# A PSUM tile each for the transposed solution and the transposed output, and two fixed tiles for the solution

## The chip, the cores and the metric

The kernel runs on one core of a Trainium2 chip. The metric is the device time of one execution in microseconds. The kernel is timed as the median of three runs; the profile is of one more execution, taken by the hardware profiler.

## The reference

Three layers follow each other on float32 data of batch 4, sequence 768 and width 320 (8 heads of 40). Only the first is touched here: a recurrent attention whose state, one 40x40 matrix for each batch and head, is updated at each of the 768 positions. The second (a gated product with a convolution of three taps) and the third (a Fourier mix, a normalisation and two products) follow it on its output.

```python
for t in range(S):
    y[:, :, t] = np.einsum('bhd,bhde->bhe', rt, state)
    Sa = np.einsum('bhde,bhe->bhd', state, at)
    state_decay = state * wt[:, :, None, :] - np.einsum('bhd,bhe->bhde', Sa, bt)
    state = state_decay + np.einsum('bhd,bhe->bhde', vt, kt)
...
h = np.maximum(x @ w_in, 0.0)
...
return (h * gate @ w_out).astype(np.float32)
...
X = np.fft.fft(x, axis=1)
X = np.fft.fft(X, axis=2)
...
ch = np.maximum(un @ w_ch1, 0.0) @ w_ch2
```

## The kernel before

The attention works on chunks of 64 positions: 12 chunks `c` and 4 batches `b`, so 48 units, one after the other. Two batches share a set of loaded tiles (`hb` is the half, `bl` the batch in it), and the heads lie in three groups of up to three heads (120 partitions). Inside a chunk the recurrence is a triangular system. Its inverse `tt` is found for eight units at a time by `inverse`, most of it on DVE: a transpose (L311), then 60 operations that each need the one before them (L331 multiplies, L334 adds; "the chain" below), then three transposes (L341 once, L344 twice), after which TensorE merges blocks in two parts, `bp` (L358) and, a step later, `mp` (L371).

`run` (L593) calls `step` (L525) 52 times. In step `n` stand, in this order, parts of several units: `u` of unit n interleaved with `hu` of unit n-3's next chunk and with `y` of unit n-2 (L530 to L539); `stage_s` (`sp`, the new state) and `stage_g` (`gp`) of unit n-1; what is prepared ahead (`joins`, which issues `bp` and `mp`, then `gram` and `xp` of a unit 15 steps on, while there are any); `stage_sb` (`ss`); `stage_ut` of unit n; `stage_o` of unit n-3. The names are those of the PSUM tiles. All tiles of PSUM come from one pool of eight buffers, each a bank of 512 float32 a partition (`pst`, L133).

`stage_ut` (L428) transposes the solution `z` of the unit by three matmuls (128x64 results) into columns 0 to 191 of the tile `ct`, and ACT copies them to `zt` (L435). `stage_o` (L499) transposes the output `ys` of an older unit into columns 192 to 383 of the same `ct`, and DVE multiplies them into `xo` (L507), which is stored. TensorE's part of most of these stages goes through `in_turn` (L382), so that its order is that of the calls. A scheduler sets the order on the other engines as it builds the program, from its own estimate of times. It also makes two instructions of different engines on one tile of PSUM wait for each other, as in program order.

`load_z` (L178) takes a new `z` from a pool with two buffers for each chunk and half, loads its upper 64 partitions and clears 40 padding columns of the lower 64 on GpSimd (L183). ACT writes the solution into the lower half (L425).

Of the kernel before, what the change touches and what calls it, by code (L numbers as in the profile page):

```python
# [10 lines left out]
F32 = mybir.dt.float32  # L11
# [9 lines left out]
C = 64  # L21
NCH = S // C
NG = 3
HG = 3
P3 = HG * D
DM = H * D
# [48 lines left out]
def turns(left, right):  # L75


    sides = []
    for stages in (left, right):
        ops = []  # L80
        for todo, end in stages:
            ops += [(op, None) for op in todo[:-1]] + [(todo[-1], end)]
        sides.append(ops)
    n = max(len(ops) for ops in sides)
    for k in range(n):
        for ops in sides:
            for op, end in ops[k * len(ops) // n:(k + 1) * len(ops) // n]:
                op()
                if end is not None:
                    end()  # L90
                    yield
# [7 lines left out]
class Attn:  # L99
    def __init__(self, ctx, tc, ins, xd):  # L100
        self.tc, self.nc, self.xd = tc, tc.nc, xd
        self.i = ins
        nc = self.nc
        cp = ctx.enter_context(tc.tile_pool(name="a_const", bufs=1))
        self.early = ctx.enter_context(tc.tile_pool(name="a_early", bufs=1, side="right"))
        self.pre = ctx.enter_context(tc.tile_pool(name="a_pre", bufs=1))
        mid = [ctx.enter_context(tc.tile_pool(name=f"a_mid{j}", bufs=1)) for j in range(2)]
        self.ps = ctx.enter_context(tc.tile_pool(name="a_ps", bufs=8, space=PSUM))
        self.ends = cp.tile([P3, 6 * 66], F32, name="ends")
        nc.vector.memset(self.ends, 0.0)  # L110
        ev = self.ends.rearrange("p (a b) -> p a b", b=66)
        nc.vector.memset(ev[:, :, 0:66:65], 1.0)
        self.stat = cp.tile([P3, 4 * NCH], F32, name="stat")
        self.abd = [cp.tile([P3, HG, 2 * NG, C], F32, name=f"abd{j}") for j in range(2)]
        self.rbd = [cp.tile([P3, HG, 2 * NG, C], F32, name=f"rbd{j}") for j in range(2)]
        self.ident = cp.tile([128, 128], F32, name="ident")
        mlt = cp.tile([128, C + 2], F32, name="mlt")
        self.mlt, self.mq = mlt[:, 0:C], mlt[:, C:C + 2]
        self.mltq = mlt
        self.mdiag = cp.tile([P3, P3], F32, name="mdiag")  # L120
        self.hbd = [cp.tile([128, 4, 2, D], F32, name=f"hbd{b}") for b in range(B)]
        self.st = [cp.tile([P3, NG, P3], F32, name=f"st{b}") for b in range(B)]
        self.sb = [cp.tile([P3, NG, P3], F32, name=f"sb{b}") for b in range(B)]
        self.ys = [self.pre.tile([64, NG * P3], F32, name=f"ys{j}") for j in range(2)]
        self.sm = [self.pre.tile([P3, NG, P3], F32, name=f"sm{j}") for j in range(1)]

        self.slots = {}
        for k, n, m, shape in (("x", 10, 4, [128, 2, NG * P3]), ("lk", 8, 4, [128, 2, 4, C]), ("tt", 2, 1, [128, 32, 64])):
            self.slots[k] = [mid[j >= m].tile(shape, F32, name=f"{k}{j}") for j in range(n)]
        self.hf, self.late, self.markd, self.lastpe = {}, None, None, None  # L130
        self.grp = {}
# [46 lines left out]
    def load_z(self, c, hb):  # L178
        nc, pre, i = self.nc, self.pre, self.i
        d = self.hf[c, hb]  # L180
        z = d["z"] = pre.tile([128, 2, NG * P3], F32, name="z", tag="z", bufs=2)
        nc.sync.dma_start(z[0:C], i["zv"][c, hb])
        nc.gpsimd.memset(z[C:128, :, DM:], 0.0)  # L183
        zt = d["zt"] = pre.tile([P3, 6, 2, C], F32, name="zt", tag="zt", bufs=2)
        nc.sync.dma_start(zt[:, :, 0], i["vt"][c, hb])
        for h in range(HG):
            nc.sync.dma_start(self.rbd[hb][D * h:D * h + D, h], i["r"][c, hb, D * h:D * h + D])
# [3 lines left out]
        self.nc.sync.dma_start(t, self.i["r"][c, hb])  # L191

    def pads(self):
        for t in self.ys:
            self.nc.gpsimd.memset(t[:, DM:], 0.0)
        for t in self.sm:
            self.nc.gpsimd.memset(t[:, 2], 0.0)
# [227 lines left out]
            self.mark = nc.scalar.mul(d["z"][64:128, bl, 0:DM], hu[0:64, 0:DM], -1.0)  # L425
        return ops, end

    def stage_ut(self, c, b, ct):  # L428
        nc = self.nc
        bl, d = b % 2, self.hf[c, b // 2]  # L430
        up = ct[:, 0:192]
        for gi in range(NG):
            self.mm_t(up[0:P3, 64 * gi:64 * gi + 64],
                                d["z"][64:128, bl, P3 * gi:P3 * gi + P3], self.ident[64:128, 64:128])
        self.mark = nc.scalar.copy(d["zt"][:, bl * NG:bl * NG + NG, 1],  # L435
                       up[0:P3, 0:192].rearrange("p (g t) -> p g t", t=C))
# [59 lines left out]
            self.mm_t(ss[0:P3, P3 * gi:P3 * gi + P3], self.st[b][:, gi], self.ident[:P3, :P3])  # L496
        nc.scalar.copy(self.sb[b].rearrange("p a b -> p (a b)"), ss[0:P3, 0:NG * P3])

    def stage_o(self, c, b, ct):  # L499
        nc, pre = self.nc, self.pre  # L500
        bl, d = b % 2, self.hf[c, b // 2]
        yt = ct[:, 192:384]
        for gi in range(NG):
            self.mm_t(yt[0:P3, 64 * gi:64 * gi + 64], d["ys", b][:, P3 * gi:P3 * gi + P3],
                                self.ident[:64, :64])
        xo = pre.tile([P3, NG, C], F32, name="xo", tag="xo", bufs=3)
        self.markd = nc.vector.tensor_tensor(xo, yt[0:P3, 0:192].rearrange("p (g t) -> p g t", t=C),  # L507
                                d["wx"][:, bl * NG:bl * NG + NG, 0:C], op=ALU.mult)
        for x, c0 in self.xd:
            if c0 <= c < c0 + x.shape[-1] // C:  # L510
                nc.sync.dma_start(x[b].rearrange("(g p) t -> p g t", p=P3)[:, :, (c - c0) * C:(c - c0 + 1) * C], xo)
# [13 lines left out]
    def step(self, n, pre):  # L525
        def at(k):
            return divmod(n - k, B) if 0 <= n - k < B * NCH else (None, None)

        left, right = [], []
        c, b = at(0)  # L530
        if c is not None:
            left.append(self.stage_u(c, b))
        c, b = at(HL)
        if c is not None and c < NCH - 1:
            left.append(self.stage_h(c + 1, b))
        c, b = at(2)
        if c is not None:
            right.append(self.stage_y(c, b))
        yield from turns(left, right)  # L539
        c, b = at(1)  # L540
        if c is not None and c < NCH - 1:
            self.stage_s(c, b)
            yield
        if c is not None:
            self.stage_g(c, b)
            if b % 2 and c + 1 < NCH:
                self.load_z(c + 1, b // 2)
            yield
        for _ in pre:
            yield  # L550
        c, b = at(3)
        if c is not None and c < NCH - 1:
            self.stage_sb(c, b)
            yield
        ct = self.pst("ct")
        c, b = at(0)
        if c is not None:
            self.stage_ut(c, b, ct)
            yield
        c, b = at(3)  # L560
        if c is not None:
            self.stage_o(c, b, ct)
            yield


# [843 lines left out]
```

## Time and profile before

| | |
|---|---|
| median of three runs | 1041.9 us (1039.63 to 1045.36) |
| profiled execution | 1041.13 us; its span, first to last instruction, 1039.3 us |
| busy share of the span | PE 82%, DVE 64%, ACT 50%, POOL 42% |
| mean granted TensorE clock | 0.901 of full speed |
| attention's steps | 72.4 to 544.5 us of the span, then the other two layers |

PE is TensorE, PEld its weight loads, DVE VectorE, ACT ScalarE, POOL GpSimd, SP the queue that issues the loads and stores. A busy share is an average over the whole span, in which the steps of the attention and the large products after it have different limits. Idle time of an engine counts only where the chain of work passes through it. Each engine works through its own queue in order, so an instruction that waits holds back all that stand behind it.

### The profile page before, as it was taken

Reading aid. Unit: us, or ns where it says so; the run is one execution under the profiler, and the core shown is the slowest. Engines: PE = TensorE matmul, PEld = TensorE weight load, DVE = VectorE, ACT = ScalarE, POOL = GpSimd, SP = SyncE. Lnnn points to the kernel's source line nnn. Section 1 sums busy time; section 2 is a strip of 40 time slices with the busy share of each in tenths; the row PEclk is TensorE's granted clock in tenths of the full one; section 3 lists DMA queues with packets and bytes.
Section 4 is the critical chain, followed back from the end, with each engine's and each line's share of the span. In section 5 each row is a group of like instructions: output and inputs, shape, how many; then the busy total and the mean of one; then the engine's idle time right before and its main releaser. Section 6 shows DMA issues by size and latency. Waiting matters only on the chain. (4 is left out here: it accounts for less than half of the span.)

```text
span 1039.3 us, 21821 instructions
## 1 busy us (share of the span) xinstructions
PE 847.6 (82%) x8178; PEld 772.4 (74%) x8178; DVE 665.1 (64%) x1320; ACT 521.5 (50%) x1448; POOL 432.2 (42%) x529
## 2 busy tenths in 40 slices
PE   4557657657867776687878999988999999999997
PEld 3446657656766675677767777776888999999997
DVE  6984965983796597296326888888875445434321
ACT  4657466556556655544337676665754331222211
POOL 5555264453445344233316776767365203101000
PEclk8668688888887888897989999999999999999999
DMA  9523335445454435252834573321304000000001
GB/s 235 167 65 88 103 110 133 138 121 137 130 153 113 114 108 141 69 148 76 246 79 116 147 221 115 96 71 33 89 2 149 30 7 20 21 20 20 20 7 36
DMA packets 102990, 101.16 MB, mean 97 GB/s; under 512 B 47272, under 2 KB 89115, under 8 KB 102875
## 3 DMA queue, kind: packets, MB, share of 16 engines
q1 hardware_dynamic: 100907, 94.73, 32.5%
q0 software_dynamic: 1968, 4.93, 1.6%
q8 instruction: 67, 1.10, 0.5%
q14 instruction: 48, 0.39, 0.1%
HBM read 74.81 MB, written 20.76 MB: 92 GB/s over the span
## 5 line engine op out<-in xcount | busy, mean ns | idle before, releaser
L877 DVE SCALAR_TENSOR_TENSOR c<-h,cw,c 128x384 f32<-128x384 f32 x128 | 110.6, 867 | 23.7 <-ACT c L875 20.9
L894 PE MATMUL acc<-w_out_f,z 128*128 128x320 f32 x384 | 114.9, 436 | 5.7 <-POOL z L881 3.0
L386 PE MATMUL ct<-ident,ys 64*120 64x64 f32 x144 | 21.2, 262 | 116.3 <-ACT zt L435 116.0
L1131 DVE SCALAR_TENSOR_TENSOR gl<-hp,gh 128x384 fp32r<-128x384 f32 x80 | 44.4, 556 | 111.3 <-ACT gh L1130 111.2
L1130 ACT ACTIVATE gh<-hp 128x384 fp32r<-128x384 f32 x80 | 39.3, 492 | 149.8 <-PE hp L700 149.6
L386 PEld LDWEIGHTS ct<-ident,ys 64*120 64x120 f32 x144 | 13.8, 154 | 122.8 <-ACT zt L435 122.2
L894 PEld LDWEIGHTS acc<-w_out_f,z 128*128 128x128 f32 x384 | 71.2, 190 | 29.4 <-POOL z L881 4.7
L700 PE MATMUL hp<-xh,w_in_h 128*128 128x386 f32 x192 | 75.8, 395 | 11.1 <-ACT h L868 11.0
L700 PE MATMUL hp<-uh,w_ch_h 128*128 128x384 f32 x240 | 82.3, 343 | 0.0
L700 PE MATMUL hp<-ul,w_ch_h 128*128 128x384 f32 x240 | 81.0, 337 | 0.0
L386 PE MATMUL yp<-x,gt 128*64 128x40 f32 x768 | 76.6, 267 | 1.6 <-DVE gt L468 1.6
L1154 POOL DMA_INDIRECT out<-o,rows x12 | 11.8, 984 | 150.7 <-DVE o L1149 131.9
L386 PEld LDWEIGHTS yp<-x,gt 128*64 128x64 f32 x768 | 72.8, 171 | 2.2 <-DVE gt L468 2.2
L1144 PE MATMUL acc<-w_ch_h,gh 128*128 128x320 f32 x240 | 73.2, 312 | 0.0
L1144 PE MATMUL acc<-w_ch_l,gh 128*128 128x320 f32 x240 | 73.0, 309 | 0.0
L217 PE MATMUL gram<-abd,kb 120*128 120x192 f32 (+1 forms) x288 | 56.4, 339 | 17.0 <-DMA abd<-a 10.5
L334 DVE TENSOR_TENSOR A<-A,tmp 128x30 f32<-128x30 f32 (+9 forms) x150 | 65.5, 437 | 3.5
L331 DVE TENSOR_TENSOR tmp<-A 128x30 f32<-128x30 f32 (+9 forms) x150 | 64.8, 432 | 3.4
L700 PE MATMUL hp<-xl,w_in_h 128*128 128x386 f32 x192 | 66.4, 346 | 0.0
L217 PEld LDWEIGHTS gram<-abd,kb 120*128 120x128 f32 x288 | 51.5, 212 | 18.8 <-POOL l L262 10.7
L455 POOL TENSOR_TENSOR st<-st,sm 120x360 f32<-120x360 f32 x40 | 41.3, 1032 | 56.9 <-DVE sm L454 53.1
L237 POOL TENSOR_TENSOR lk<-lk,mlt 128x256 f32<-128x256 f32 x48 | 37.7, 786 | 61.3 <-ACT lk L236 60.9
(225 smaller groups left out, 2703.4 us busy)
## 6 DMA issues: line engine op xcount, KB each, us to landing
kb<-in_kb SPq DMA_DIRECT2D x24, 360.0 KB
vbd<-in_vbd SPq DMA_DIRECT2D x24, 320.0 KB
xd<-xo SPq DMA_DIRECT2D x56, 90.0 KB
w<-in_w SPq DMA_DIRECT2D x24, 185.6 KB
a<-in_a SPq DMA_DIRECT2D x24, 180.0 KB
z<-in_zv SPq DMA_DIRECT2D x24, 180.0 KB
zt<-in_vt SPq DMA_DIRECT2D x24, 180.0 KB
rbd<-in_r SPq DMA_DIRECT2D x72, 60.0 KB
```

What stands on the lines that cost most here:

```text
L217: nc.tensor.matmul(gp[:, 192 * gi:192 * gi + 64 * nh], d["kb"][:, bl * NG + gi].rearrange("p a b -> p (a b)"), abd[:, 0:nh, bl * NG + gi], ...
L237: nc.gpsimd.tensor_tensor(d["lk"][:, bl], d["lk"][:, bl], self.mlt.unsqueeze(1).to_broadcast([128, 4, C]), op=ALU.mult)
L331: nc.vector.tensor_tensor(tmp, A[:, s + 1:32, s:s + 1].to_broadcast([128, n, s]), A[:, s:s + 1, 0:s].to_broadcast([128, n, s]), op=ALU.mult)
L334: nc.vector.tensor_tensor(A[:, s + 1:32, 0:s], A[:, s + 1:32, 0:s], tmp, op=ALU.add)
L386: self.lastpe = op(*args, **kw)
L455: nc.gpsimd.tensor_tensor(self.st[b], self.st[b], t, op=ALU.add)
L700: nc.tensor.matmul(out, l, r, start=(j == 0), stop=(j == len(ops) - 1))
L877: nc.vector.scalar_tensor_tensor(c, h[:, j:HS + j], cw[:, f, j:j + 1], c, op0=ALU.mult, op1=ALU.add)
L894: nc.tensor.matmul(self.acc[t][:, 0:DM], z[:, ts], w[:, f], start=(f == 0), stop=(f == NF1 - 1))
L1130: self.mark = nc.scalar.activation(gh, hp[:, 0:HS], AF.Relu)
L1131: nc.vector.scalar_tensor_tensor(gl, hp[:, 0:HS], 0.0, gh.bitcast(F32), op0=ALU.max, op1=ALU.subtract)
L1144: nc.tensor.matmul(self.acc[t][:, 0:DM], l[:, ts], r, start=(f == 0 and j == 0), stop=(f == NF2 - 1 and j == 2))
```

## The change

The shared tile `ct` becomes two, `up` and `yt`, one for each stage. The tiles of `z` are two fixed ones, one for each half, whose padding is cleared once (`pads`) and no longer for each chunk and half.

```diff
+        self.z = [self.pre.tile([128, 2, NG * P3], F32, name=f"z{j}") for j in range(2)]
...
-        z = d["z"] = pre.tile([128, 2, NG * P3], F32, name="z", tag="z", bufs=2)
+        z = d["z"] = self.z[hb]
         nc.sync.dma_start(z[0:C], i["zv"][c, hb])
-        nc.gpsimd.memset(z[C:128, :, DM:], 0.0)
...
     def pads(self):
+        for t in self.z:
+            self.nc.gpsimd.memset(t[C:128, :, DM:], 0.0)
...
-    def stage_ut(self, c, b, ct):
+    def stage_ut(self, c, b):
...
-        up = ct[:, 0:192]
+        up = self.pst("up")
...
-    def stage_o(self, c, b, ct):
+    def stage_o(self, c, b):
...
-        yt = ct[:, 192:384]
+        yt = self.pst("yt")
...
-        ct = self.pst("ct")
```

In the attention the order on PE stays; what changes there is what its instructions wait for. This is PE's queue at the end of a step without a merge, before (the last row but one of a step's transposes is `ct<-ident,ys`, then the next step begins with `u`):

```order
L253 MATMUL xp<-ident,kb 128x120 x2
L386 MATMUL ss<-ident,st_103 120x120 [waits DVE_49]
L386 MATMUL ss<-ident,st_103 120x120 x2
L386 MATMUL ct<-ident,z 120x64 [waits Activation_49]
L386 MATMUL ct<-ident,z 120x64 x2
L386 MATMUL ct<-ident,ys_109 120x64 [waits Activation_49]
L386 MATMUL ct<-ident,ys_109 120x64 x2
L386 MATMUL u<-hbd_99,tt_130 64x80 [waits PE_49]
```

And the same place in the changed kernel (lines are two further down):

```order
L255 MATMUL xp<-ident,kb 128x120 x3
L388 MATMUL ss<-ident,st_103 120x120 x3
L388 MATMUL up<-ident,z_111 120x64 [waits Activation_49]
L388 MATMUL up<-ident,z_111 120x64 x2
L388 MATMUL yt<-ident,ys_109 120x64 [waits PE_49,Activation_49]
L388 MATMUL yt<-ident,ys_109 120x64 x2
L388 MATMUL u<-hbd_99,tt_132 64x80 [waits Activation_49]
```

Nothing moved. The wait of `ct<-ident,ys` on ACT was for the copy L435 of this same step; that of `yt` is for the bank that it takes over, which `hu` of this step held until ACT's copies of it (L410, in the new file L412). `u` takes the bank of `yp`, and waits for ACT's copy L487 (now L489) of this step.

The scheduler orders DVE anew. Here is the end of the third chain (that of `tt_129`) on DVE before, from the store's multiplication `xo` on; `bp` of this chain is issued on PE a step later:

```order
L331 TENSOR_TENSOR tmp<-A 128x30
L334 TENSOR_TENSOR A<-A,tmp 128x30
L507 TENSOR_TENSOR xo<-ct,wx 120x192
L164 SCALAR_TENSOR_TENSOR wx<-w,ends 120x396
L341 STREAM_TRANSPOSE t_3872<-A 128x32x32
L344 STREAM_TRANSPOSE tt_129<-A 128x32x32 x2
L163 RECIPROCAL ends<-vx 120x6
L450 TENSOR_TENSOR sm_110<-sp,mdiag 120x240
L454 TENSOR_TENSOR sm_110<-sp,mdiag 80x80
```

And the end of the same chain in the change (L313 for L311, L333, L336, L343, L346 for L331, L334, L341, L344), which now lies in the very step in which PE issues `bp`; `gt` of that step stands four rows ahead of the first row here:

```order
L336 TENSOR_TENSOR A<-A,tmp 128x5x26
L333 TENSOR_TENSOR tmp<-A 128x108
L336 TENSOR_TENSOR A<-A,tmp 128x4x27
L333 TENSOR_TENSOR tmp<-A 128x84
L336 TENSOR_TENSOR A<-A,tmp 128x3x28
L333 TENSOR_TENSOR tmp<-A 128x58
L336 TENSOR_TENSOR A<-A,tmp 128x2x29
L333 TENSOR_TENSOR tmp<-A 128x30
L336 TENSOR_TENSOR A<-A,tmp 128x30
L343 STREAM_TRANSPOSE t_3870<-A 128x32x32
L346 STREAM_TRANSPOSE tt_131<-A 128x32x32 x2
L509 TENSOR_TENSOR xo<-yt,wx 120x192
```

The chain's 60 operations, counted between one `xo` and the next, were 2, 15, 12, 16 and 15 before, with the three last transposes in the sixth interval, a step ahead of `bp`. They are 7, 10, 8, 9, 7 and 19 now, with the transposes in the sixth interval too, now behind the last 19. The second and fourth chains moved in the same way.

At the same `bp` PE's queue reads, before:

```order
L386 MATMUL gp<-rbd_91,zt 128x192 [waits PE_49]
L386 MATMUL gp<-rbd_91,zt 128x192
L386 MATMUL gp<-rbd_91,zt 128x128
L386 MATMUL bp<-t_3872,l_2263 32x32 [waits PE_49]
L386 MATMUL bp<-t_3872,l_2263 32x32 x31
```

And in the change:

```order
L388 MATMUL gp<-rbd_91,zt 128x192 [waits Activation_49]
L388 MATMUL gp<-rbd_91,zt 128x192
L388 MATMUL gp<-rbd_91,zt 128x128
L388 MATMUL bp<-t_3870,l_2261 32x32 [waits DVE_49]
L388 MATMUL bp<-t_3870,l_2261 32x32 x63
```

`gp` now waits for ACT itself (the copy to `zt`), and `bp` for DVE's transpose.

## Rows read from the trace of the kernel before

**Rows 1.** Windows: the steps' time; us, busy (instructions) by engine, clock, DMA share, GB/s

```profile
72.40:544.50 472.10, 342.09 (x5000) 314.51 (x4999) 310.83 (x658) 261.93 (x812) 201.02 (x252) 0.83 0.45 122
```

**Rows 2.** Waits of PE, 100 to 540 us: total us, times, longest

```profile
PE ct L386 <- ACT zt L435: 116.0, 45, 7.9
PE bp L386 <- DVE t L341: 3.1, 1, 3.1
```

**Rows 3.** Timeline, one step: start, us, engine, operation, idle before and its releaser

```profile
259.00 0.57 PE L386 MATMUL ct<-ident,ys 64*120 64x64 f32 x3 [4.84 <-ACT zt L435]
...
263.54 1.08 PE L386 MATMUL gp<-rbd,zt 120*128 120x192 f32 x6
...
263.83 0.17 POOL L183 MEMSET z<- 64x80 f32 x1 [2.41 <-PE sp L386]
...
268.46 0.34 ACT L435 COPY zt<-ct 120x192 f32<-120x192 f32 x1
...
268.85 0.39 PE L386 MATMUL ct<-ident,ys 64*120 64x64 f32 x3 [2.43 <-ACT zt L435]
```

**Rows 4.** Windows: five stretches from L311 to `bp`, the end, and a chain alone

```profile
103.75:144.45 40.70, 28.03 (x342) 26.08 (x342) 36.88 (x80) 23.31 (x72) 16.11 (x18) 0.71 0.35 98
177.17:237.65 60.48, 38.91 (x430) 36.02 (x430) 54.58 (x113) 34.12 (x110) 31.03 (x38) 0.83 0.48 135
267.00:324.85 57.85, 41.29 (x430) 38.07 (x430) 53.32 (x112) 32.66 (x108) 29.71 (x38) 0.82 0.48 133
354.45:411.55 57.10, 38.45 (x430) 35.62 (x430) 51.46 (x109) 32.35 (x108) 28.13 (x37) 0.85 0.46 121
439.84:480.99 41.15, 31.47 (x449) 28.10 (x450) 38.53 (x102) 19.27 (x57) 16.48 (x22) 1.00 0.53 144
480.99:544.50 63.51, 51.59 (x806) 46.66 (x806) 18.66 (x40) 23.79 (x60) 16.99 (x24) 0.81 0.49 134
...
177.17:228.10 50.93, 33.73 (x370) 31.18 (x370) 48.87 (x101) 28.30 (x91) 24.00 (x28) 0.87 0.51 145
```

**Rows 5.** Timeline: the third chain's last transposes on DVE, and its `bp` on PE

```profile
314.24 3.62 DVE L344 STREAM_TRANSPOSE tt<-A 128x1024 f32<-128x1024 f32 x2
324.85 2.21 PE L386 MATMUL bp<-t,l 32*32 32x32 f32 x128
```

**Rows 6.** Timeline: neighbouring chain operations of one size, and GpSimd beside them

```profile
271.75 0.27 DVE L331 TENSOR_TENSOR tmp<-A 128x108 f32<-128x108 f32 x1
271.90 1.69 POOL L175 TENSOR_TENSOR kb<-kb,vx 120x768 f32<-120x768 f32 x1 [3.36 <-DMA kb<-in_kb]
272.05 1.66 DVE L334 TENSOR_TENSOR A<-A,tmp 128x108 f32<-128x108 f32 x1
```

**Rows 7.** Windows of the chain's operations alone (tile `tmp`), second and last stretch

```profile
177.17:237.65 60.48, 26.32 (x60) 0.83 0.48 135
...
439.84:480.99 41.15, 22.73 (x60) 1.00 0.53 144
```

**Rows 8.** Timeline: PE's transposes of `ys` between the stretches, with their waits

```profile
157.13 0.57 PE L386 MATMUL ct<-ident,ys 64*120 64x64 f32 x3 [6.75 <-ACT zt L435]
...
244.56 0.39 PE L386 MATMUL ct<-ident,ys 64*120 64x64 f32 x3 [2.70 <-ACT zt L435]
...
430.75 0.57 PE L386 MATMUL ct<-ident,ys 64*120 64x64 f32 x3 [2.69 <-ACT zt L435]
```

**Rows 9.** Timeline: waits in the last steps

```profile
502.10 0.39 PE L386 MATMUL ct<-ident,ys 64*120 64x64 f32 x3 [0.45 <-ACT zt L435]
522.31 0.83 ACT L838 CAST xh<-xf 128x772 fp32r<-128x772 f32 x1 [7.09 <-DMA xf<-xd]
524.32 0.57 PE L386 MATMUL ct<-ident,ys 64*120 64x64 f32 x3 [7.87 <-ACT zt L435]
```

**Rows 10.** Windows: two steps with a merge, at two levels of the clock

```profile
418.46:430.75 12.29, 9.60 (x202) 8.90 (x202) 2.65 (x7) 7.39 (x21) 2.98 (x4) 0.83 0.22 53
486.41:497.17 10.76, 10.31 (x194) 9.66 (x194) 2.17 (x8) 4.41 (x10) 3.22 (x7) 0.60 0.22 52
```

More of the change, by code (lines that the diff above doesn't have):

```diff
@@ L554, in step @@
             yield
-        ct = self.pst("ct")
         c, b = at(0)
         if c is not None:
-            self.stage_ut(c, b, ct)
+            self.stage_ut(c, b)
             yield
@@ L561, in step @@
         if c is not None:
-            self.stage_o(c, b, ct)
+            self.stage_o(c, b)
             yield
```

## The prediction

> **What bounds the kernel now.** I read the windows first, to see where the time lies: the attention's steps take 472.10 us, and PE is busy for 342.09 of them at a granted clock of 0.83 [rows 1]. The rest of the program, nearly as long, is not touched. The view of waits then says what PE's idle time in the steps is: 116.0 us in 45 waits, all of one kind, TensorE's transposes of `ys` into `ct` waiting for ACT's copy of the other half of `ct` to `zt`; the next kind is 3.1 us [rows 2].
>
> The timeline of one step shows the mechanism. PE gets to the transposes of `ys` with all their data there, but ACT has the copies of `gram`, `xp` and `ss` ahead of the copy to `zt`, which starts at 268.46; PE goes on at 268.85, after 2.43 us of nothing [rows 3]. `ys` itself was copied in the step before. So the wait is one for the tile, not for data.
>
> A third view warns against taking 116 us as the gain. DVE's chain (60 dependent operations and four transposes) is issued in stretches, from L311 to the `bp` that needs it. In the middle of such a stretch DVE is busy for 48.87 of 50.93 us, 96% [rows 4]: PE waits for ACT there, but DVE has next to no time left either. I cut the steps, therefore, into the five stretches of a chain and what lies between, and ask of each what ends last in it once PE no longer stops.
>
> **The change part by part.**
>
> *The stretches of a chain.* All that DVE does from L311 to `bp` must still be done, but for the two transposes L344, which only the later `mp` needs (3.62 us) [rows 5]. In the second stretch that leaves 54.58 - 3.6 = 51.0 us of DVE in 60.48, in the third 53.32 - 3.6 = 49.7 in 57.85, in the fourth 51.46 - 3.6 = 47.9 in 57.10 [rows 4]. At the 96% they become 53.1, 51.8 and 49.9: gains of 7.4, 6.1 and 7.2 us, 20.7 in sum. Where does it come from? In the third, the transposes end at 314.24 + 3.62 = 317.9 and `bp` starts at 324.85 [rows 5]: 7 us in which the chain is done and DVE idles. The new order spreads the chain into that step. I take 14 of the 20.7: 2.3 a stretch go off because every second step also has two scans on DVE, so that in the others PE, not DVE, ends last. The bounds are 0 (PE waits at `bp` for all that it gained) and 20.7.
>
> The first and last stretches have no such slack: DVE is busy for 36.88 of 40.70 and 38.53 of 41.15 us [rows 4], and the 3.1 us of `bp` waiting for DVE lie in the last [rows 2]. At 96% they would give 2.3 and 1.0 us; I take 1 for both, bounds 0 and 3.3.
>
> *Between the stretches.* Here PE and ACT rule. Eight of the waits lie in the four pieces from `bp` to the next L311: 6.75, 4.84 and six of 2.69 to 2.71 us, 27.8 in sum [rows 3, 8]. `gp` of the next step needs the same copy to `zt`, so the wait is not gone, it is put off: to be free it must be shorter than what PE does from `yt` to `gp`. That took from 259.00 to 263.54, 4.54 us [rows 3]. Six waits and almost all of the 4.84 fit under it; 2.2 us of the 6.75 and 0.3 of the 4.84 are left, so 25.3 us are gained.
>
> Something goes back. A chain whose last operations come in the step of `bp` leaves PE idle at `bp`: in the third stretch 11 of them stand behind `gt`, at 26.32 / 60 = 0.44 us [rows 7], and a transpose of half of 3.62 [rows 5], some 7 us. How a long pause is paid for shows in the last merge: after the wait at `bp` a step with a merge has PE busy for 10.31 us at a clock of 0.60, where another has 9.60 at 0.83 [rows 10], though more of its records are there. I take 4 us off, one for each piece: 21. Bounds: 27.8, and 12, if ACT's copies make PE wait at `gp` for half.
>
> *The last steps*, 480.99 to 544.5 us. Seven waits are of about 0.45 us [rows 9], one is 7.87. That one is ACT's, which itself waits 7.09 us for the next layer's first load before it can copy to `zt` [rows 9]; no tile of PSUM moves that load. PE's cover lets it do 4.54 us of work meanwhile at best, and what the short waits give ahead of the load is lost at it. I take 3, bounds 0 and 3 + 4.5 = 7.5.
>
> *The padding.* 24 clearings of 0.17 us become two. POOL waits at each until `sp` has read the tile, 2.41 us in this row [rows 3]; behind it in POOL's queue stands the state's update, which waits for DVE's product of the same `sp`. So it costs nothing now and gains nothing; what covers it is that wait, and without the cover it would be worth 22 x 0.17 = 3.7 us of POOL, an engine with room. Two fixed `z` change no data's path: the load of a `z` waited for the same readers before.
>
> *The tenth tile.* A step takes ten tiles of PSUM now, not nine, from eight buffers. `yt` mostly takes the bank of `hu`, whose copies are over some 5 us earlier; I cost it at nothing. If that cover is gone (ACT late with `hbd`), PE waits at `yt` for ACT again, which is the rival of no change below.
>
> *A rule on DVE and GpSimd.* A chain operation on 108 columns took 0.27 us, and the next one of that size 1.66, while GpSimd's product of 1.69 us ran [rows 6]. So DVE's busy time above holds time in which it was held. If the new order freed the chain of that, its 26.32 us in the second stretch would fall to the 22.73 of the last, where GpSimd has less to do [rows 7]. I keep it as it is, since GpSimd's products are all still there in a shorter stretch, and price the other case as a rival. The Trainium skill says it of the units themselves (GPSIMD Engine Reference, Specifications): GpSimd shares its SBUF interfaces with VectorE, and the two contend when a VectorE instruction has two SBUF inputs. By that rule a denser queue meets GpSimd no less often, and the sum stands; the trace agrees on the one pair.
>
> *The sum*: 14 + 1 + 21 + 3 = 39 us. The profiled execution took 1041.1 us (span 1039.3 and 1.8 around it), 0.8 under the median of the runs shown. 1041.1 - 39 = 1002 us.
>
> **The rivals.**
>
> *DVE is held less.* The chain's operations shrink to the size of the last stretch, 3.6 us a stretch and 11 in the three, and the 7 us for the scans do not come off. For it: PE's pause was never DVE's limit, and the scheduler fills DVE with what is ready. Against it: rows 6. 1002 - 18 = 984 us.
>
> *The wait moves to `bp`.* Chain stretches take as long as before, and only the rest is gained: 21 + 3 = 24, 1017 us. For it: the change's order puts 19 operations and the transposes into the step of `bp`, behind `gt`, where before they were done a step ahead. Against it: DVE's sum allows it to be done sooner.
>
> *No change*: PE waits at `gp` or `yt` for as long as it did, since ACT's queue from one `zt` to the next is the loop that ends last. Against it: ACT is busy for 34.12 of 60.48 us [rows 4]. 1040 us.
>
> *Slower*: DVE, ordered by estimates, holds PE up at each step (`gt` and the mask product behind chain operations, `bp` behind all 60), and the stretches get longer. The point from which it decides: the 25 us gained elsewhere are lost if the three long stretches grow by 8 us each, which is DVE busy for 51.0 of 68.5, 74% and not 96%. At 14 us each: 1041 - 25 + 42 = 1058 us.
>
> *All of the 116 us*: only if DVE bound nothing; rows 4 exclude it, and I give it no chance of its own.
>
> **How the numbers follow.** Forecast 0.50 (its own range 990 to 1014 us, from the bounds of the terms taken singly), DVE held less 0.15, the wait at `bp` 0.20, no change 0.06, slower 0.09. A difference of 0.5%, 5 us, is about what a measurement of this kernel can tell from none. Faster by more: 0.50 + 0.15 + 0.20 = 0.85; within: 0.06; slower: 0.09. For eight in ten I leave out no change and slower (0.15) and the far end of the first rival: 968 to 1030 us, the low end being 984 less what the upper bounds between the stretches and at the end give beyond the values taken (6.8 and 4.5 us) and 5 us for the clock.
>
> **What would show it.** In the profile after, PE's waits for the copy to `zt` should be under 15 us, at `gp` and not at the transposes. New waits of PE for DVE should stand at `bp`, 6 to 10 us each in the second to fourth chains. Those stretches should take 54 to 56, 52 to 55 and 50 to 53 us with DVE busy for 93% or more, and the four pieces between them some 21 us less in sum. The time after the steps should be as before, 495 us. The forecast is wrong if DVE's busy share in a stretch falls under 85%, if PE waits step by step for `gt` or the mask product, or if the chain's operations get much shorter than 0.44 us.

## The result, and the profile of the changed kernel

The change took the median from 1043.05 us (four runs, 1039.63 to 1045.36) to 1006.75 us (four runs, 1002.62 to 1009.25): a ratio of 0.9651, 95% interval 0.9607 to 0.9694. The forecast was 1002 us, range 968 to 1030. The profiled execution of the change took 1006.97 us, its span 1005.0 us.

The view of waits of TensorE (PE), 100 to 505 us of the changed kernel: total us, times, longest. It answers [rows 2].

```profile
PE bp L388 <- DVE t L343: 50.8, 5, 12.4
PE sp L388 <- DVE xo L509: 12.9, 9, 3.8
PE yp L388 <- DVE gt L470: 7.2, 11, 1.3
PE gp L388 <- DVE xo L509: 6.0, 3, 2.6
...
PE gp L388 <- ACT zt L437: 1.9, 4, 1.2
```

The 116.0 us at the transposes of `ys` are gone. Of the wait for the copy to `zt` 1.9 us are left, at `gp`, where the prediction put it. The largest wait is now for VectorE, at `bp`, and there are five of it. One step shows why the transposes no longer stop; the timeline's columns are start, us, engine, operation:

```profile
335.64 0.27 PE L388 MATMUL up<-ident,z 64*120 64x64 f32 x1
335.65 0.27 PE L388 MATMUL yt<-ident,ys 64*120 64x64 f32 x1
...
338.99 0.34 ACT L437 COPY zt<-up 120x192 f32<-120x192 f32 x1
```

`yt` is issued beside `up`; ScalarE's copy to `zt` comes 3.3 us later, and PE is in the next step by then.

The windows are cut as in [rows 4]: a stretch from L313 to its `bp`, then the piece to the next L313, and so on, with the last steps from 446.46 and the rest of the program in the last row. Columns: window, its length, busy us (and instructions) of PE, PEld, DVE, ACT, POOL, granted clock, DMA share, GB/s.

```profile
103.58:148.29 44.71, 23.98 (x275) 22.09 (x275) 41.68 (x87) 23.46 (x73) 18.93 (x20) 0.72 0.42 116
148.29:173.17 24.88, 23.74 (x459) 22.30 (x460) 13.48 (x23) 20.87 (x64) 13.08 (x14) 0.82 0.41 117
173.17:230.37 57.20, 33.94 (x406) 30.31 (x402) 54.58 (x115) 33.78 (x111) 33.31 (x34) 0.87 0.60 168
230.37:255.15 24.78, 22.22 (x438) 20.61 (x440) 12.19 (x19) 17.22 (x52) 10.79 (x12) 0.82 0.36 102
255.15:309.61 54.46, 35.24 (x419) 31.82 (x413) 51.87 (x112) 32.30 (x108) 31.75 (x35) 0.89 0.58 160
309.61:331.23 21.62, 21.51 (x438) 20.01 (x440) 12.04 (x21) 17.18 (x53) 11.76 (x13) 0.81 0.34 90
331.23:381.66 50.43, 33.62 (x417) 30.23 (x413) 47.81 (x110) 31.88 (x108) 27.77 (x34) 0.91 0.59 162
381.66:403.04 21.38, 21.22 (x438) 19.78 (x440) 9.69 (x18) 16.20 (x49) 7.88 (x10) 0.82 0.26 67
403.04:446.46 43.42, 29.31 (x436) 26.20 (x433) 40.67 (x107) 19.15 (x57) 18.18 (x22) 0.93 0.53 139
...
446.46:505.12 58.66, 48.55 (x806) 44.55 (x807) 16.10 (x34) 23.66 (x60) 14.59 (x18) 0.79 0.54 149
505.12:1005.00 499.88, 469.80 (x2657) 426.52 (x2657) 295.71 (x548) 220.69 (x518) 192.84 (x226) 0.99 0.21 63
```

The reader is to see two kinds of row. In the stretches DVE is busy for 93 to 95% and PE for 54 to 68%; in the pieces between them PE is busy for 90 to 99% and DVE for about half. The two engines take turns at being the limit. Against [rows 4], and the pieces that lie between their rows (32.72, 29.35, 29.60 and 28.29 us):

| us | before | change | gained | predicted |
|---|---|---|---|---|
| second to fourth stretch | 175.43 | 162.09 | 13.3 | 14 |
| first and last stretch | 81.85 | 88.13 | -6.3 | 1 |
| four pieces between | 119.96 | 92.66 | 27.3 | 21 |
| last steps | 63.51 | 58.66 | 4.9 | 3 |
| after the steps | 494.8 | 499.88 | -5.1 | 0 |

The steps gave 39.2 us, and the sum had 39; but two terms of it are off by 7.3 and 6.3 us in opposite directions, so that this agreement is in part luck. The 5 us by which the forecast missed lie behind the steps.

One wait is new and easily overlooked. `sp` waits for DVE's `xo` nine times. It reads nothing of `xo`: its data are `x` and `z`, both from ACT. In the program `sp` takes over the bank that `yt` of the step before held, and `xo` empties that bank:

```profile
264.07 0.43 ACT L427 ACTIVATE z<-u 64x320 f32<-64x320 f32 x1
...
265.13 0.34 DVE L509 TENSOR_TENSOR xo<-yt,wx 120x192 f32<-120x192 f32 x1
...
265.53 0.82 PE L388 MATMUL sp<-z,x 128*120 128x120 f32 x6 [3.02 <-DVE xo L509]
```

`z` is done at 264.50, `xo` at 265.47, and `sp` starts 0.05 us later; in all nine waits it starts 0.05 or 0.06 us behind `xo`. Beyond the end of `z` they come to 7.2 of the 12.9 us. This, too, is a wait for a bank and not for data, in the stretches in which VectorE is full.

### The profile page after: what moved, and what is told of

Same layout as the page of the kernel before. It is cut to its first block, busy times and chain, and to the rows that moved or that the text cites. A ratio compares the mean times of both kernels' runs of the same rounds, so it can differ in the third digit from the quotient of the medians.

```text
span 1005.0 us, 21806 instructions
## 1 busy us (share of the span) xinstructions
PE 824.0 (82%) x8178; PEld 748.7 (75%) x8178; DVE 670.5 (67%) x1320; ACT 518.4 (52%) x1448; POOL 437.7 (44%) x507
## 5 line engine op out<-in xcount | busy, mean ns | idle before, releaser
L1131 ACT ACTIVATE gh<-hp 128x384 fp32r<-128x384 f32 x80 | 39.2, 491 | 149.9 <-PE hp L701 149.7
L895 PEld LDWEIGHTS acc<-w_out_f,z 128*128 128x128 f32 x384 | 71.3, 190 | 28.2 <-POOL z L882 3.4
L701 PE MATMUL hp<-xh,w_in_h 128*128 128x386 f32 x192 | 76.1, 396 | 15.5 <-ACT h L869 15.5
L219 PE MATMUL gram<-abd,kb 120*128 120x192 f32 (+1 forms) x288 | 63.8, 371 | 16.9 <-DMA abd<-a 10.9
L457 POOL TENSOR_TENSOR st<-st,sm 120x360 f32<-120x360 f32 x40 | 43.5, 1087 | 70.8 <-DVE sm L456 47.8
L219 PEld LDWEIGHTS gram<-abd,kb 120*128 120x128 f32 x288 | 58.3, 235 | 19.0 <-issue 11.3
L388 PE MATMUL yp<-x,gt 128*64 128x40 f32 x768 | 63.6, 240 | 7.9 <-DVE gt L470 7.2
L333 DVE TENSOR_TENSOR tmp<-A 128x30 f32<-128x30 f32 (+9 forms) x150 | 68.1, 454 | 3.0
L388 PE MATMUL gp<-rbd,zt 120*128 120x192 f32 (+1 forms) x288 | 57.8, 341 | 13.4 <-DVE xo L509 6.0
L336 DVE TENSOR_TENSOR A<-A,tmp 128x30 f32<-128x30 f32 (+9 forms) x150 | 64.9, 433 | 2.6
L388 PE MATMUL bp<-t,l 32*32 32x32 f32 x768 | 21.2, 233 | 55.4 <-DVE t L343 50.8
L388 PEld LDWEIGHTS yp<-x,gt 128*64 128x64 f32 x768 | 58.5, 144 | 10.8 <-DVE gt L470 10.4
L879 ACT ACTIVATE c<-c 128x384 f32<-128x384 f32 x64 | 33.4, 521 | 61.0 <-DVE c L878 60.8
```

Of the source, the lines that this page charges most:

```text
L219: nc.tensor.matmul(gp[:, 192 * gi:192 * gi + 64 * nh], d["kb"][:, bl * NG + gi].rearrange("p a b -> p (a b)"), abd[:, 0:nh, bl * NG + gi], ...
L333: nc.vector.tensor_tensor(tmp, A[:, s + 1:32, s:s + 1].to_broadcast([128, n, s]), A[:, s:s + 1, 0:s].to_broadcast([128, n, s]), op=ALU.mult)
L336: nc.vector.tensor_tensor(A[:, s + 1:32, 0:s], A[:, s + 1:32, 0:s], tmp, op=ALU.add)
L388: self.lastpe = op(*args, **kw)
L457: nc.gpsimd.tensor_tensor(self.st[b], self.st[b], t, op=ALU.add)
L701: nc.tensor.matmul(out, l, r, start=(j == 0), stop=(j == len(ops) - 1))
```

## The experiments

Theory: PE's stop at `ct` set the pace of the long stretches and of what lies between them; with it gone, the stretches take as long as VectorE's work in them takes. The rivals differ from one experiment to the next and stand in the expectations. Times are medians; each ratio is to runs of the kernel before on the same chip.

### One part of the change at a time

The tiles split, but `z` as before (`split_only`):

```diff
-        z = d["z"] = self.z[hb]
+        z = d["z"] = pre.tile([128, 2, NG * P3], F32, name="z", tag="z", bufs=2)
         nc.sync.dma_start(z[0:C], i["zv"][c, hb])
+        nc.gpsimd.memset(z[C:128, :, DM:], 0.0)
```

> The two PSUM tiles as in the change, but z from the pool of two with its padding cleared for each chunk and half, as before. Theory (all of the gain is PE no longer stopped at the transposes of ys; the padding is nothing): 1003 to 1011 us, the same as the change within 0.5%. Rival (the fixed z, whose clearings and waits leave GpSimd's queue, carries a part): 1012 to 1030 us.

Measured: 1007.23 us, ratio 0.9669 (0.9640 to 0.9697).

The fixed `z` alone, with `ct` for both stages (`z_only`):

```diff
-        z = d["z"] = pre.tile([128, 2, NG * P3], F32, name="z", tag="z", bufs=2)
+        z = d["z"] = self.z[hb]
         nc.sync.dma_start(z[0:C], i["zv"][c, hb])
-        nc.gpsimd.memset(z[C:128, :, DM:], 0.0)
```

> One tile ct for both stages as before, but two fixed z with the padding cleared once. Theory: 1039 to 1046 us, no change, and PE's waits for the copy to zt still 110 to 120 us. Rival (the fixed z carries a part): 1015 to 1035 us.

Measured: 1043.7 us, ratio 1.0003 (0.9985 to 1.0020); the waits at `ct` for the copy to `zt` are 113.1 us. All of the gain is the second PSUM tile's. With the tile VectorE's order changes too, as the scheduler sets it anew; no run has two tiles and the order of before, so what the order adds by itself is not shown.

### Half a chain, with two tiles and with one

```diff
-            for s in range(1, 31):
+            for s in range(1, 16):
```

> The change with the chain of the five later groups cut to its first 30 of 60 operations (the second half of the inverse's elimination is left out, some 13 us of VectorE a chain); all else is there. Theory (with two tiles the stretches of a chain are VectorE-full): the waits at bp, 50.8 us in the change, fall under 15, and 955 to 975 us. Rival (TensorE and ScalarE end last in a stretch anyway): 990 to 1005 us.

> The kernel before with the same half of the chain left out. Theory (with the shared tile TensorE's stop at ct, 116 us in all, sets the pace of the three long stretches, and VectorE that of the first and last alone): 1022 to 1043 us, waits for the copy to zt still 100 to 120 us, so that the change is worth 55 to 85 us without the chain's second half, not 36. Rival (half a chain is worth the same with either tile): 990 to 1010 us, difference of the two 30 to 42 us.

Measured: 947.59 us with two tiles, ratio 0.9082 (0.9056 to 0.9107); 1041.57 us with one, ratio 0.9995 (0.9970 to 1.0020). The second to fourth stretches, first with two tiles, then with one:

```profile
161.20:207.35 46.15, 36.11 (x406) 32.98 (x402) 43.73 (x79) 33.50 (x110) 28.64 (x29) 0.89 0.66 183
...
228.12:271.85 43.73, 35.18 (x418) 31.72 (x412) 42.28 (x79) 32.44 (x108) 28.42 (x33) 0.92 0.60 165
...
291.44:338.64 47.20, 36.05 (x418) 33.13 (x413) 39.94 (x78) 31.35 (x106) 27.38 (x34) 0.86 0.54 145
```

```profile
175.42:231.93 56.51, 38.99 (x429) 36.10 (x429) 42.02 (x83) 34.04 (x110) 28.58 (x38) 0.85 0.55 146
...
260.98:320.36 59.38, 42.26 (x430) 39.05 (x430) 41.36 (x82) 32.65 (x108) 28.40 (x38) 0.80 0.49 132
...
344.19:402.75 58.56, 40.91 (x430) 37.92 (x430) 36.34 (x79) 32.63 (x108) 26.97 (x37) 0.83 0.45 118
```

With one tile VectorE lost 12 to 15 us of work in each stretch, and the three take 174.5 us in sum where [rows 4] have 175.4: VectorE idles for a quarter of them and more, and PE still waits 110.6 us at `ct`. With two tiles they shrink by 11, 11 and 3 us, and no wait of these chains at `bp` is left. Without half of the chain the change is worth 94 us, with it 36. This is the plainest sign that the stop at `ct` was the limit before, and VectorE is after.

The whole time hides something here. With one tile the last transposes of `ys` come at 535.93 us instead of 544.68, 8.7 us earlier, but the part behind them, which no edit touches, took 6.6 us longer in that execution. Up to the last transposes of `ys` the change is worth 86.7 us without half of the chain and 39.4 with it. In the third of the stretches with two tiles VectorE is busy for 85% only, so there it is no longer the limit alone. The 947.59 us lie under my 955 to 975, and the 94 us above my 55 to 85: I had not reckoned that the first and last stretch would shrink as well (to 33.65 and 34.41 us), nor the four pieces, which went from 92.66 to 81.52 us in sum.

### VectorE's work spread over more of the period

The chain can't start before its last `gram`, and must end at `bp`. Three edits widen that: `gram` a step earlier ("early"), two steps earlier ("early2"), and the merge a step later ("late").

```diff
-LG = 15
+LG = 16
...
-NA = 7
+NA = 8
```

> The change, with gram and xp prepared 16 steps ahead and not 15 (and one more double step at the start), so that a chain may start a step earlier; its order has the 60 operations over seven intervals and not six, and 0 to 12 of them in the step of bp where 15 to 20 were. Theory (the stretch of a chain is DVE-full, and the 51 us of PE waiting at bp are the chain's tail): the bp waits fall under 20 us in sum, 965 to 985 us. Rival (DVE is not the limit, the loop over PE and ACT ends last anyway, and a wait of the same size shows up elsewhere): 998 to 1010 us.

> The kernel before with the same earlier preparation. Theory (with the shared tile, PE's stop at ct sets the pace in the three long stretches, DVE has slack there): 1033 to 1046 us, PE's waits for zt still over 105 us. Rival (a chain's early start is worth the same with either tile): 1000 to 1015 us.

With `LG = 17` and `NA = 9`:

> The change with gram and xp 17 steps ahead (two more double steps at the start); by its order the chain's last transposes stand one to three intervals ahead of bp. Theory (VectorE is the limit over the whole period, its busy time grows as its operations meet GpSimd's more often, as with 16 steps, where the chain of the second stretch took 32.7 us and not 27.0): the bp waits fall under 15 us, but only 980 to 993 us. Rival (the bp waits are all a matter of order, and go): 955 to 975 us. Rival (no gain past 16 steps, the queues of loads end last): 993 to 1005 us.

```diff
-            for last, m in (("merge", v["end"] - 2), ("join", v["end"] - 1)):
+            for last, m in (("merge", v["end"] - 1),):
```

> The change with the merge a step later: bp in the step before its first unit, mp at that unit's step ahead of its u. The chain itself starts where it did; by its order the last 19, 20 and 15 operations of the three long chains now lie over two or three intervals and the transposes an interval later. Theory (TensorE waits at bp since the chain's tail comes in that step; VectorE fills its idle time of the next step instead): the bp waits, 50.8 us, fall to 10 to 25, u waits 1 to 3 us a merge for ScalarE's copies, 978 to 993 us. Rival (VectorE is full and the same wait shows up at another instruction): 1000 to 1010 us.

> The kernel before with the same later merge. Theory (its chains were done a step ahead of bp, TensorE waited there for 3.1 us in all): 1040 to 1055 us, not faster. Rival (a later merge gains with either tile): 1015 to 1030 us.

Both edits together, `LG = 16` and the later merge:

> The change with both: gram and xp 16 steps ahead, as in the run of that alone (994.95 us), and the merge a step later. By its order no chain operation lies in the step of bp in the three long chains. Theory (VectorE's work spread over the whole period leaves bp no wait): bp waits under 12 us, 965 to 985 us. Rival (the chain only grows longer beside GpSimd, which took 5.6 us in one stretch with 16 steps): 990 to 1000 us.

> The kernel before with both the earlier preparation and the later merge, which took the change from 1006.75 to 976.75 us. Theory (with the shared tile TensorE's stop at ct ends last in every step, so VectorE's order is worth nothing): 1042 to 1056 us, waits at ct for the copy to zt still over 100 us. Rival (the order is worth some 30 us with either tile): 1008 to 1022 us.

| | one tile `ct` | two tiles |
|---|---|---|
| as it was | 1 | 0.9651 (0.9607 to 0.9694) |
| early | 1.0060 (1.0029 to 1.0090) | 0.9540 (0.9518 to 0.9563) |
| late | 1.0050 (1.0031 to 1.0070) | 0.9616 (0.9575 to 0.9657) |
| early2 | not run | 0.9800 (0.9764 to 0.9836) |
| late and early | 1.0088 (1.0060 to 1.0116) | 0.9353 (0.9334 to 0.9372) |

In us, with two tiles: 994.95, 1005.08, 1022.26 and 976.75; with one: 1050.32, 1049.27 and 1052.07.

With one tile every one of these made the kernel slower by 0.5 to 0.9%, early more than my range allowed. Part of that lies behind the steps: the last transposes of `ys` come 5.4, 4.6 and 6.8 us later than in the kernel before (early, late, both). With two, early and late together took another 30 us off, as the theory expected, and that is a version faster than both kernels. Alone each fell short. Early gave 12 us where I expected 22 to 42, so it lies between its theory and its rival. Late gave 2 where I expected 14 to 29, which its interval does not tell from none, and lies in its rival's range. The waits at `bp` are still 34.2 and 40.0 us. In early the chain also grew: in the second stretch it ran beside GpSimd's products for 20.6 us, where it had for 14.7 in the change, and took longer. The windows of the chain's operations alone (tile `tmp`), second stretch, of the change and then of early:

```profile
173.17:230.37 57.20, 27.04 (x60) 0.87 0.60 168
```

```profile
171.82:233.24 61.42, 32.68 (x60) 0.93 0.65 173
```

Early2 missed all three of its ranges. Its third rival named the right thing, a queue of loads that ends last, but priced it at no gain and not at a loss: with `gram` in the very step in which `a` is loaded into `abd` (L175), PE waits for that load. The view of waits:

```profile
PE gram L219 <- DMA abd<-a: 60.8, 11, 10.8
```

Late and early together leave one wait at `bp`, of 7.8 us. The stretch and the piece behind it are best read together there. Second and third:

```profile
164.40:229.83 65.43, 51.63 (x694) 47.31 (x689) 63.67 (x127) 47.60 (x151) 41.32 (x43) 0.90 0.63 170
229.83:235.44 5.61, 5.61 (x239) 5.34 (x240) 4.33 (x10) 4.37 (x14) 4.20 (x5) 1.00 0.47 149
235.44:298.05 62.61, 49.34 (x622) 44.86 (x616) 60.73 (x122) 44.67 (x146) 35.79 (x39) 0.92 0.59 165
298.05:304.33 6.28, 6.24 (x266) 5.93 (x267) 4.94 (x10) 6.04 (x18) 6.20 (x9) 1.00 0.37 106
```

A period of 81.98 us in the change (57.20 + 24.78) is 71.04 here, and VectorE is busy for 68.0 of it, 96%: nearly no time is left in which it waits for its turn.

### GpSimd beside VectorE

Three of GpSimd's products are left out from chunk 2 on: `kb` by `vx`, `a` by `wx`, the mask on `lk`.

```diff
-        self.markp = nc.gpsimd.tensor_tensor(kb, kb, vx[:, :, 2:66].unsqueeze(2).to_broadcast([P3, 6, 2, C]), op=ALU.mult)
+        if c < 2:
+            self.markp = nc.gpsimd.tensor_tensor(kb, kb, vx[:, :, 2:66].unsqueeze(2).to_broadcast([P3, 6, 2, C]), op=ALU.mult)
```

and the same for the other two.

> The change without three of GpSimd's products from chunk 2 on (kb by vx, a by wx and the mask on lk are left out, 48 of its 107 us in 173 to 382 us of the changed kernel); VectorE's order is the same but for one row. Theory (VectorE's operations on two tiles are held while GpSimd works): the chain's 60 operations take under 24.5 us in the second to fourth stretches, where they took 27.0, 27.6 and 29.0 (22.5 in the last, where GpSimd is busy for 18 of 43 us), and 975 to 995 us. Rival (their length has nothing to do with GpSimd): 26 to 29 us each, 1000 to 1008 us.

Measured: 970.5 us, ratio 0.9303 (0.9278 to 0.9327), below the 975 to 995 of the theory. (GpSimd is busy for some 115 us from 173 to 382 us of the change, not 107; the three products are 48 of them.) The chain alone (tile `tmp`) in the five stretches, of the change and of this kernel:

```profile
103.58:148.29 44.71, 26.84 (x60) 0.72 0.42 116
...
255.15:309.61 54.46, 27.64 (x60) 0.89 0.58 160
331.23:381.66 50.43, 28.97 (x60) 0.91 0.59 162
403.04:446.46 43.42, 22.51 (x60) 0.93 0.53 139
```

```profile
100.73:138.84 38.11, 22.59 (x60) 0.81 0.52 137
163.74:213.92 50.18, 23.24 (x60) 0.89 0.74 191
237.00:283.64 46.64, 21.83 (x60) 0.90 0.66 186
305.30:348.92 43.62, 23.22 (x60) 0.93 0.66 179
370.28:413.70 43.42, 22.51 (x60) 0.93 0.52 140
```

The last stretch, in which only one of these products stood (0.7 us), is the control: 43.42 us and 22.51 in both. In the others the same 60 operations are 3.8 to 5.8 us shorter. The groups of VectorE's instructions in the second stretch, of the change and of this kernel (us busy, mean ns of one):

```profile
L752 DVE TENSOR_TENSOR wl<-pm,wh 128x256 fp32r<-128x256 f32 x5 | 4.7, 943 | 0.0
L470 DVE TENSOR_TENSOR gt<-gp,mlt 128x512 f32<-128x512 f32 x6 | 4.1, 680 | 0.0
L336 DVE TENSOR_TENSOR A<-A,tmp 128x234 f32<-128x234 f32 x2 | 2.6, 1316 | 0.0
L452 DVE TENSOR_TENSOR sm<-sp,mdiag 120x240 f32<-120x240 f32 x6 | 2.4, 400 | 0.0
...
L780 DVE TENSOR_SCALAR pm<-pm 128x256 int32<-128x256 int32 x5 | 3.0, 595 | 0.0
```

```profile
L473 DVE TENSOR_TENSOR gt<-gp,mlt 128x512 f32<-128x512 f32 x6 | 4.1, 680 | 0.0
L755 DVE TENSOR_TENSOR wl<-pm,wh 128x256 fp32r<-128x256 f32 x5 | 2.7, 531 | 0.9 <-DMA w_in_l<-wl 0.9
L455 DVE TENSOR_TENSOR sm<-sp,mdiag 120x240 f32<-120x240 f32 x6 | 2.4, 401 | 0.0
L339 DVE TENSOR_TENSOR A<-A,tmp 128x234 f32<-128x234 f32 x2 | 0.8, 396 | 0.0
...
L783 DVE TENSOR_SCALAR pm<-pm 128x256 int32<-128x256 int32 x5 | 1.5, 309 | 0.0
```

Of what reads two tiles of SBUF, `wl` and part of the chain are shorter; what reads one of PSUM and one of SBUF (`gt`, `sm`) is as it was to 1 ns. The Trainium skill (GPSIMD Engine Reference, Specifications) states contention on the shared SBUF interfaces for VectorE instructions in a 2-port perf mode or with two SBUF inputs. The trace agrees for `wl`, 943 against 531 ns. Two SBUF inputs are not the whole of it in this trace: L780, which reads one tile of SBUF, went from 595 to 309 ns. In all, VectorE's 115 instructions of this stretch went from 54.58 us to 46.22 and the stretch from 57.20 to 50.18, while PE's waits at `bp` stayed at 51.3 us: a wait's size told nothing of what could be had there.

The first four stretches gave 28.2 of the 36 us. The products left out also stood in the path of data to `gram` and `hu`, so that not all of the 36 us need be VectorE's; and the kernel with one tile was not run without them.

## Why the prediction was right, and where its terms were off

*The stop at `ct`.* Right: it was one for the tile. The waits for `zt` fell from 116.0 to 1.9 us, and splitting the tile alone gives all of the gain.

*The 116 us can't be had, since VectorE fills up.* Right, and shown from both sides: the same split is worth 94 us where VectorE has half a chain less to do.

*The three long stretches.* 14 predicted, 13.3 measured: 57.20, 54.46 and 50.43 us where I expected 54 to 56, 52 to 55 and 50 to 53, so the first is longer than I said. VectorE is busy for 95%, and the 96% read in the middle of one stretch was the right measure for all. That the term came out is in part luck. VectorE had 54.58, 51.87 and 47.81 us to do, and the working had 51.0, 49.7 and 47.9, which is 5.7 us less in sum. The 6.9 us taken off for the scans stood in for that; their own reason, that TensorE ends last in every second step, is not shown by a VectorE that is busy for 95%. The reading "7 us in which the chain is done and DVE idles" was wrong as well: of the 6.99 us from 317.86 to 324.85 DVE was busy for 3.97.

*The first and last stretch.* This step failed: 1 us predicted, 6.3 lost, outside the term's bounds of 0 and 3.3. I held VectorE's work in a stretch fixed. But a stretch ends where `bp` stands among VectorE's instructions, and the new order put more ahead of it: 87 instructions and 41.68 us where there were 80 and 36.88, and 107 and 40.67 for 102 and 38.53 [rows 4]. The stretches grew by 4.0 and 2.3 us, the work by 4.8 and 2.1. These are the waits at `bp` of 10.3 and 10.4 us that I had only in the middle three.

*Between the stretches.* 21 predicted, 27.3 measured, near the upper bound of 27.8. The 4 us taken off for the clock were not due in sum, though the price behind a pause is there. In the 5.3 to 5.6 us behind the pauses at the second to fourth `bp` the granted clock is 0.50, the lower of its two levels, 1.2 of 2.4 GHz, with TensorE busy throughout; behind the third it is 0.73 in the next 5 us and 1.00 after that. The working left out that before, with the stops at `ct`, the clock had been low in these pieces too: 1.00 right behind the second and third `bp`, but 0.58 from 255 to 261 us and 0.51 from 331 to 337. Over whole pieces it was 0.84, 0.83, 0.77 and 0.82 before, and is 0.82, 0.82, 0.81 and 0.82. Some of the first piece's 7.8 us is the work that moved into the first stretch, so this term and the last one belong together: 21.0 where I had 22.

*The wait at `bp`.* I put 6 to 10 us each into the second to fourth chains. They are 12.4, 8.9 and 8.8. Here is the longest, in the timeline:

```profile
226.87 1.26 POOL L338 TENSOR_SCALAR_AFFINE_SELECT A<-A 128x1024 f32<-128x1024 f32 x1 [3.38 <-DVE A L336]
228.19 0.16 POOL L340 MEMSET A<- 128x32 f32 x1
228.38 1.93 DVE L343 STREAM_TRANSPOSE t<-A 128x1024 f32<-128x1024 f32 x1 [1.59 <-POOL A L340]
...
230.37 0.36 PE L388 MATMUL bp<-t,l 32*32 32x32 f32 x5 [12.37 <-DVE t L343]
```

I had added the chain's last operations and half a transpose. Missing was the hop to GpSimd between them (L338, L340), in which VectorE idles for 1.59 us. The rival "the wait moves to `bp`" named the right place: the wait did appear there, and the stretches gained all the same.

*The last steps, the padding, the tenth tile.* 4.9 us for 3; the padding 0, as in `z_only`. PE waits at `yt` for under 1 us in all, but the tenth tile was not free: the bank of `yt` makes `sp` wait for `xo`, 7.2 us beyond its data, where I had looked for ACT at `yt` alone. Those waits lie in VectorE-full stretches; what they cost by themselves was not tried.

*VectorE held by GpSimd.* Kept as it was, and right in the sum: the chain took 27.04, 27.64 and 28.97 us in the three stretches where it had taken 26.3 to 28.2. But the experiment shows the size of what I had left at one pair of rows: 36 us of the whole time hang on three of GpSimd's products.

*After the steps.* "As before, 495 us" failed by 5.1. In the window 555.52 to 580.52 us PE is busy for 18.43 us of 25 at a clock of 0.93 (before, as far behind the steps, from 594.90 on: 22.59 us at 1.00), and the waits of `hp` for ScalarE went from 11.0 to 15.5 us. From the last `yt` or `ct` transpose on, the kernels with one tile took 493.6 to 501.2 us, and those with two 498.9 to 501.8. So a part that the edit doesn't touch varies by some 8 us between the profiled executions of these programs. What sets it was not tried and stays open.

*The forecast's own range.* The 990 to 1014 us do not follow from the bounds: the terms taken singly give 995 to 1016.

## What to carry to other kernels

Two uses of one tile by two engines make a wait with no data behind it; a step that takes one tile more from the same banks can make another. Before pricing its removal, cut the time into the stretches in which another engine is nearly full, and price each by that engine's busy time; then ask which of its instructions the new order puts ahead of the next place where the first engine waits. A full engine's busy time is itself a variable: look for a neighbour that lengthens its instructions, and try an order that spreads its work over the whole period, which here paid only once the false wait was gone.

## What the runs showed of the hardware

The size of the hold between GpSimd and VectorE was not expected: 14.5 us of GpSimd's products less in the second stretch (three groups of 5.8, 5.5 and 3.2 us in the change) made VectorE's busy time there 8.4 us shorter. Single operations differ by a factor: 1316 against 396 ns for the mean of two on 234 columns.
